# Linear attention feeding a gated FFN on one core: the order of every engine's instructions is chosen by the Tile scheduler instead of being the order of emission

## Chip, cores and metric

One NeuronCore of one Trainium2 chip runs the whole program. The metric is the device time of one execution in microseconds (us), lower is better. The profile is one execution taken by the hardware profiler.

## What is computed

Eight batches of eight heads, 576 tokens, head size 64, go through linear attention; the result, 4608 tokens of 512 features, goes through a feed-forward block whose two first products are multiplied element by element.

```
phi(x) = where(x > 0, x, exp(x) - 1) + 1
kv  = einsum('bhsd,bhse->bhde', phi(k), v);   z = sum over s of phi(k)
x   = einsum('bhsd,bhde->bhse', phi(q), kv) / (phi(q) . z + 1e-6)     # then (4608, 512)
out = (((x @ w1) * (x @ w2)) @ w3) @ w_out                            # 512 -> 1024 -> 1024 -> 512
```

Inputs and output are float32.

## The kernel before, in words

The matmuls run in bfloat16. Since nothing stands between `w3` and `w_out`, the kernel first forms their product `wf` (1024 x 512) on the chip: eight times `wf_unit` (eight transposes into the PSUM tile w3p, a copy to `w3t` on ScalarE, eight matmuls into `wf_ps`, a copy out on ScalarE).

Attention goes batch by batch. `load_qkv` brings k, v and q of a batch (1 MB each plus two small pieces for the last 64 tokens) through SyncE's queue (SP) into a pool `ld` of six buffers, which the float32 weights use too. `phi_steps` computes phi: two Exp instructions on ScalarE (line 127), two minima on VectorE (line 128), then four and one scalar_tensor_tensor on VectorE (lines 133 and 138) that write kj and kr, or qj and qr; the pool of these has one buffer each. `v_steps` casts v into `vt` on VectorE. `kv_unit` multiplies phi(k) with v (20 matmuls into `kvp`) and VectorE writes `kvz`; `tr_unit` (three parts) transposes phi(q) into `tp`, and VectorE copies it to `qt`; `nd_unit` (four) and `ndr_unit` (one, for the last 64 tokens) form numerator and denominator in `nd`; `nd_finish` computes exp(-ln(d)) in two ScalarE instructions (lines 230 and 231) and multiplies on VectorE (line 232) into `xt`, the transposed input of the FFN. kvp, tp, nd and w3p share a PSUM pool of two buffers (`at`).

The FFN goes in nine chunks of 512 tokens. `f_unit(c, f)`, written F(c,f) below, with f from 0 to 7, makes four matmuls into `a_ps` and four into `b_ps` (line 265), a copy of a_ps on ScalarE (line 268) and a product on VectorE into `ab` (line 269). `o_unit(c, m)`, written O(c,m), with m from 0 to 3, makes eight matmuls of ab with wf into `o_ps` (line 275), a copy on ScalarE (line 278) and a store from SP's queue (lines 282 and 285). a_ps, b_ps, o_ps and wf_ps share a PSUM pool of four buffers (`mm`).

Chunk c can start when all the columns of xt that it reads are written; the attention of batch c+1 is emitted among the units of chunk c, and the phi steps of batch c+2 between the later units. Up to chunk 5 this is the pattern. Chunk 6 still holds the attention of the last batch, but no phi steps; chunks 7 and 8 hold F and O units alone. The order written by hand for a chunk is:

```
units = [F(0), KV, F(1), O(0), T(0), T(1), F(2), T(2), O(1), F(3), N(0), F(4), N(1),
         O(2), F(5), N(2), F(6), N(3), NR, O(3), F(7)]      # O(m) is of chunk c-1
```

The beginning is written out too: weights of the product wf, then batch 0, then F(0,0) to F(0,7) with the phi steps of batch 1's k and its v cast between the last four, then the q steps of batch 1, its kv and tr units, O(0,m) and nd units in turn, and then the loads of batch 2 followed by all its phi steps, before F(1,0).

Line 75 sets `tc.manual_schedule()`: the instructions of each engine, and the DMAs on SP's queue, stand in the order in which this Python code emits them. Each engine takes its own list in order and waits at an instruction until that one's inputs and buffers are there. Semaphores between engines are generated from the data dependencies.

Of the kernel before, what the change touches and what calls it, by code (L numbers as in the profile page):

```python
# [18 lines left out]
def kernel(  # L19
# [52 lines left out]
    mm_ps = ctx.enter_context(tc.tile_pool(name="mm_ps", bufs=4, space=bass.MemoryType.PSUM))  # L72
    at_ps = ctx.enter_context(tc.tile_pool(name="at_ps", bufs=2, space=bass.MemoryType.PSUM))

    ctx.enter_context(tc.manual_schedule())
    nc.scalar.preload_act_table_set("natural_log_exp_and_others")

    ident = consts.tile([P, P], BF16)
# [377 lines left out]
```

## Time and profile before

| | |
|---|---|
| median of 3 runs | 342.56 us (342.13 to 477.45) |
| profiled execution, its own time | 344.31 us |
| its span, first to last instruction | 342.5 us |
| TensorE busy with matmuls (PE) | 278.5 us, 81% |
| VectorE (DVE) | 172.8 us, 50% |
| ScalarE (ACT) | 155.2 us, 45% |
| GpSimd (POOL) | 12.5 us, 4% |
| mean granted TensorE clock | 0.893 of full speed |
| read from HBM, written to it | 38.80 MB, 9.44 MB |

The span is 1.8 us shorter than the profiled execution's own time, since the time has work around the first and last instruction in it. Matmuls are pipelined, so a busy PE may still run at half its clock; the granted clock has to be read beside it. One execution of the three was far slower than the other two.

### The profile page before, as it was taken

Reading aid. Unit: us, or ns where it says so; the run is one execution under the profiler, and the core shown is the slowest. Engines: PE = TensorE matmul, PEld = TensorE weight load, DVE = VectorE, ACT = ScalarE, POOL = GpSimd, SP = SyncE. Lnnn points to the kernel's source line nnn. Section 1 sums busy time; section 2 is a strip of 40 time slices with the busy share of each in tenths; the row PEclk is TensorE's granted clock in tenths of the full one; section 3 lists DMA queues with packets and bytes.
Section 4 is the critical chain, followed back from the end, with each engine's and each line's share of the span. In section 5 each row is a group of like instructions: output and inputs, shape, how many; then the busy total and the mean of one; then the engine's idle time right before and its main releaser. Section 6 shows DMA issues by size and latency. Waiting matters only on the chain.

```text
span 342.5 us, 3960 instructions
## 1 busy us (share of the span) xinstructions
PE 278.5 (81%) x1440; PEld 128.6 (38%) x1440; DVE 172.8 (50%) x306; ACT 155.2 (45%) x237; POOL 12.5 (4%) x26
## 2 busy tenths in 40 slices
PE   1747484986962894998899699969988999999995
PEld 0223241434421441443354245424433544444442
DVE  1235264389226888349356935873494444232220
ACT  2153506270533395169228633942692256333332
POOL 2400430000000000000000000000000000000000
PEclk9989865795886797899699989989998999999999
DMA  7999953000179992020194049108700002010123
GB/s 267 398 356 380 373 154 124 2 2 0 61 225 363 325 298 94 3 61 31 41 324 142 33 146 330 34 30 265 243 31 31 33 31 61 33 62 32 63 61 122
DMA packets 47539, 48.49 MB, mean 142 GB/s; under 512 B 14240, under 2 KB 38816, under 8 KB 47520
## 3 DMA queue, kind: packets, MB, share of 16 engines
q1 hardware_dynamic: 47520, 48.24, 42.6%
q8 instruction: 11, 0.18, 0.2%
q14 instruction: 8, 0.07, 0.1%
HBM read 38.80 MB, written 9.44 MB: 141 GB/s over the span
## 4 chain that ended last, share of the span: by engine, by line
PE 74%; DVE 11%; ACT 6%; DMA 5%; issue 3%; SPq 0%; DVEq 0%; ACTq 0%
PE o_ps L275 20%; PE a_ps L265 19%; PE b_ps L265 18%; PE wf_ps L298 5%; PE nd L238 3%; PE kvp L182 3%; DVE qj L133 3%; DMA w<-in_moe_w_out_dram 3%; PE tp L211 2%; ACT w3t L295 2%; DMA k<-in_k_dram 2%; ACT e L127 2%; DVE xt L232 2%; PE kvp L188 1%; DVE ab L269 1%
## 5 line engine op out<-in xcount | busy, mean ns | idle before, releaser
L265 PEld LDWEIGHTS <-w_sb 128*128 128x128 bf16 x576 | 58.1, 103 | 77.9 <-issue 17.0
L269 DVE TENSOR_TENSOR ab<-a_sb,b_ps 128x512 bf16<-128x512 f32 x72 | 49.2, 684 | 75.4 <-PE b_ps L265 75.4
L265 PE MATMUL a_ps<-xt,w_sb 128*128 128x512 bf16 x288 | 81.2, 408 | 4.1 <-DVE xt L232 2.3
L265 PE MATMUL b_ps<-xt,w_sb 128*128 128x512 bf16 x288 | 77.5, 393 | 0.1
L275 PE MATMUL o_ps<-wf_sb,ab 128*128 128x512 bf16 x288 | 74.5, 408 | 0.0
L268 ACT COPY a_sb<-a_ps 128x512 f32<-128x512 f32 x72 | 41.9, 582 | 61.2 <-PE a_ps L265 55.4
L278 ACT COPY o_sb<-o_ps 128x512 f32<-128x512 f32 x36 | 21.0, 584 | 59.4 <-PE o_ps L275 59.4
L275 PEld LDWEIGHTS <-ab 128*128 128x128 bf16 x288 | 28.7, 103 | 35.4 <-issue 6.5
L230 ACT ACTIVATE r<-nd,eps 128x512 f32<-128x512 f32 (+1 forms) x40 | 25.7, 644 | 23.5 <-PE nd L248 13.0
L232 DVE TENSOR_TENSOR xt<-nd,r 128x512 bf16<-128x512 f32 (+1 forms) x40 | 25.3, 633 | 19.7 <-ACT r L231 19.5
L128 DVE TENSOR_SCALAR e<-e 128x1152 bf16<-128x1152 bf16 x32 | 14.4, 454 | 36.9 <-ACT e L127 36.8
L298 PE MATMUL wf_ps<-wo_sb,w3t 128*128 128x512 bf16 x64 | 20.3, 460 | 14.4 <-ACT w3t L295 12.3
L231 ACT ACTIVATE r<-r 128x512 f32<-128x512 f32 (+1 forms) x40 | 23.5, 587 | 1.3
L182 PE MATMUL kvp<-vt,kj 128*128 128x130 bf16 x128 | 15.5, 251 | 10.4 <-DVE vt L163 10.4
L238 PE MATMUL nd<-qt,kvz 128*128 128x512 bf16 x64 | 20.5, 409 | 2.9 <-DVE xt L232 2.3
L133 DVE SCALAR_TENSOR_TENSOR qj<-q,e 128x512 bf16<-128x512 f32 x32 | 21.6, 724 | 0.3
L133 DVE SCALAR_TENSOR_TENSOR kj<-k,e 128x512 bf16<-128x512 f32 x32 | 20.9, 685 | 0.2
L127 ACT ACTIVATE e<-q 128x1152 bf16<-128x1152 f32 x16 | 18.2, 1157 | 5.2 <-DMA q<-in_q_dram 5.2
L127 ACT ACTIVATE e<-k 128x1152 bf16<-128x1152 f32 x16 | 18.2, 1163 | 5.1 <-DMA k<-in_k_dram 5.1
L248 PE MATMUL nd<-qt,kvz 128*128 128x64 bf16 x64 | 3.7, 209 | 18.2 <-DVE xt L232 18.1
L298 PEld LDWEIGHTS <-w3t 128*128 128x128 bf16 x64 | 6.4, 110 | 25.1 <-ACT w3t L295 14.9
L182 PEld LDWEIGHTS <-kj 128*128 128x128 bf16 x128 | 9.2, 109 | 15.9 <-DVE vt L163 8.4
(39 smaller groups left out, 131.8 us busy)
## 6 DMA issues: line engine op xcount, KB each, us to landing
w<-in_moe_w_dram SPq DMA_DIRECT2D x8, 1024.0 KB, 9.3
k<-in_k_dram SPq DMA_DIRECT2D x8, 1024.0 KB, 7.1
v<-in_v_dram SPq DMA_DIRECT2D x8, 1024.0 KB, 7.9
q<-in_q_dram SPq DMA_DIRECT2D x8, 1024.0 KB, 7.0
out_dram<-o_sb SPq DMA_DIRECT2D x32, 256.0 KB, 2.3
w<-in_moe_w_out_dram SPq DMA_DIRECT2D x2, 1024.0 KB, 8.5
k<-in_k_dram SPq DMA_DIRECT2D x16, 64.0 KB, 6.4
v<-in_v_dram SPq DMA_DIRECT2D x16, 64.0 KB, 6.4
```

The source lines that it names most:

```text
L127: nc.scalar.activation(out=e[:, s], in_=x[:, s], func=AF.Exp)
L133: nc.vector.scalar_tensor_tensor(out=dst_j[:, j, :].rearrange("p (h d) -> p h d", h=H), in0=xj, scalar=1.0, in1=ej, op0=ALU.add, op1=ALU.max)
L182: nc.tensor.matmul(o, kj[:, j, hp * P:(hp + 1) * P], vt[:, j, 2 * hp:2 * hp + 2, :].rearrange("p h e -> p (h e)"), start=(j == 0), stop=False)
L230: nc.scalar.activation(out=r, in_=d_ap, func=AF.Ln, bias=eps[:, 0:1])
L231: nc.scalar.activation(out=r, in_=r, func=AF.Exp, scale=-1.0)
L232: nc.vector.tensor_tensor(out=dst, in0=n_ap, in1=r, op=ALU.mult)
L238: nc.tensor.matmul(nd[:, i, :], t[:, hp, i, :], qt[:, hp, 0:NJ * P], start=True, stop=True)
L265: nc.tensor.matmul(ps, w[:, kc, f * P:(f + 1) * P], xt[:, kc, cs], start=(kc == 0), stop=(kc == KC - 1))
L268: nc.scalar.copy(out=a_sb, in_=a_ps)
L269: nc.vector.tensor_mul(out=abs_[c][:, f, :], in0=a_sb, in1=b_ps)
L275: nc.tensor.matmul(o_ps, ab[:, f, m * P:(m + 1) * P], wf_sb[:, f, :], start=(f == 0), stop=(f == FC - 1))
L298: nc.tensor.matmul(ps, w3t[:, kc, :], wo_sb[:, kc, :], start=(kc == 0), stop=(kc == FC - 1))
```

## The change

The line that fixes the order is taken out. The Tile scheduler then chooses the order at build time: engine by engine, it takes among the instructions whose inputs it reckons to be ready, and for whose tile a buffer is free, the one that was emitted earliest, with the start times that its own model of durations gives. The lists that come out are fixed in the program: at run time each engine still takes its list in order. Tiles, pools, buffer numbers, instructions and their shapes are the same.

```
@@ -72,7 +72,7 @@
     mm_ps = ctx.enter_context(tc.tile_pool(name="mm_ps", bufs=4, space=bass.MemoryType.PSUM))
     at_ps = ctx.enter_context(tc.tile_pool(name="at_ps", bufs=2, space=bass.MemoryType.PSUM))
 
-    ctx.enter_context(tc.manual_schedule())
+    pass
     nc.scalar.preload_act_table_set("natural_log_exp_and_others")
```

## Rows read from the trace of the kernel before

**Rows 1.** The page, parts 1 and 2: busy time, and two lines in 40 slices.

```profile
PE 278.5 (81%) x1440; PEld 128.6 (38%) x1440; DVE 172.8 (50%) x306; ACT 155.2 (45%) x237; POOL 12.5 (4%) x26
...
PEclk9989865795886797899699989989998999999999
DMA  7999953000179992020194049108700002010123
```

**Rows 2.** The chain that ended last, in order of time: start, duration, what.

```profile
59.66 1.89 PE a_ps L265 x4
...
134.70 1.71 PE a_ps L265 x4
...
168.38 1.71 PE a_ps L265 x4
...
262.22 1.06 PE a_ps L265 x4
...
288.39 0.86 PE a_ps L265 x4
...
331.56 6.92 PE o_ps L275 x32
```

**Rows 3.** Windows by stage: stretch, its length, busy by engine, then clock, DMA share, GB/s.

```profile
59.66:98.38 38.72, 32.50 (x152) 14.83 (x153) 22.03 (x42) 16.81 (x26) 0.00 (x0) 0.81 0.09 31
98.38:134.70 36.32, 22.56 (x113) 10.04 (x113) 26.26 (x50) 17.27 (x23) 0.00 (x0) 0.79 0.93 290
134.70:168.38 33.68, 30.34 (x154) 13.82 (x152) 20.36 (x37) 16.99 (x27) 0.00 (x0) 0.85 0.08 25
168.38:199.66 31.28, 27.94 (x154) 13.12 (x152) 19.38 (x35) 16.69 (x26) 0.00 (x0) 0.94 0.47 147
...
230.94:262.22 31.28, 27.94 (x153) 13.12 (x152) 19.38 (x35) 16.69 (x26) 0.00 (x0) 0.94 0.45 147
262.22:288.39 26.17, 26.16 (x153) 12.65 (x152) 10.86 (x17) 12.78 (x22) 0.00 (x0) 1.00 0.12 41
```

**Rows 4.** Timeline of the beginning: start, duration, engine, instruction, idle before and its releaser.

```profile
18.84 4.30 SPq L107 DMA_DIRECT2D q<-in_q_dram  x2
...
36.22 2.29 POOL L361 CAST w_sb<-w 128x512 bf16<-128x512 f32 x4 [23.22 <-DMA w<-in_moe_w_dram]
...
38.56 2.22 ACT L127 ACTIVATE e<-q 128x1152 bf16<-128x1152 f32 x2
...
41.74 3.59 PE L298 MATMUL wf_ps<-wo_sb,w3t 128*128 128x512 bf16 x8 [3.25 <-ACT w3t L295]
```

**Rows 5.** DMA issues by line: size of one, median us from issue to landing.

```profile
q<-in_q_dram SPq DMA_DIRECT2D x8, 1024.0 KB, 7.0
```

**Rows 6.** Waits of SP's queue: us in total, times, longest.

```profile
SPq L102 <- DVE qr L138: 7.1, 1, 7.1
```

**Rows 7.** Timeline from the end of chunk 0 to the start of chunk 1.

```profile
78.51 0.37 PE L182 MATMUL kvp<-vt,kj 128*128 128x130 bf16 x2 [2.49 <-DVE vt L163]
...
96.26 0.39 SPq L102 DMA_DIRECT2D k<-in_k_dram  x1
...
98.38 1.65 PE L265 MATMUL a_ps<-xt,w_sb 128*128 128x512 bf16 x4 [2.31 <-DVE xt L232]
...
103.02 2.22 ACT L127 ACTIVATE e<-k 128x1152 bf16<-128x1152 f32 x2 [5.14 <-DMA k<-in_k_dram]
...
109.26 0.40 PE L182 MATMUL kvp<-vt,kj 128*128 128x130 bf16 x2 [7.52 <-DVE vt L163]
...
110.45 2.22 ACT L127 ACTIVATE e<-q 128x1152 bf16<-128x1152 f32 x2 [5.22 <-DMA q<-in_q_dram]
```

**Rows 8.** Timeline of the end of chunk 3.

```profile
192.51 1.90 DVE L133 SCALAR_TENSOR_TENSOR qj<-q,e 128x512 bf16<-128x512 f32 x3
...
195.86 0.68 DVE L232 TENSOR_TENSOR xt<-nd,r 128x512 bf16<-128x512 f32 x1
...
196.60 0.39 PE L248 MATMUL nd<-qt,kvz 128*128 128x64 bf16 x8 [3.34 <-DVE xt L232]
```

More of the change, by code (lines that the diff above doesn't have):

```diff
@@ L73 @@
     at_ps = ctx.enter_context(tc.tile_pool(name="at_ps", bufs=2, space=bass.MemoryType.PSUM))
-    ctx.enter_context(tc.manual_schedule())
+    pass
     nc.scalar.preload_act_table_set("natural_log_exp_and_others")
```

## Prediction

> **What bounds the kernel now.** I read the page first. PE is busy for 81% of the span, VectorE for 50%, ScalarE for 45% [rows 1]: TensorE sets the pace, and no other engine is near full. But the busy share is not evenly spread, and neither is the granted clock: the PEclk line falls to 5 in the seventh slice (51 to 60 us) and to 5 and 6 near 94 and 103 us, and has 9s at the end [rows 1]. The DMA line is full up to about 43 us, empty from about 60 to 86, and full again from 94 to 128 [rows 1]: loads stop in the middle of the ramp and then come in a burst.
>
> Next the chain that ended last, which is PE nearly throughout. I use it as a ruler. F(c,7) closes each written-out chunk, and its a_ps starts at 134.70 (c = 1), 168.38 (2), then at 262.22 (5) and 288.39 (6) [rows 2]; 199.66 and 230.94 lie between. Windows cut at these points show what a chunk costs [rows 3]. From 262.22 to 288.39 the work is eight F, four O and one batch's attention, and PE is busy for 26.16 of 26.17 us at clock 1.00. The chunks before it (168.38 to 199.66, 230.94 to 262.22) hold the same PE work, 152 weight loads in each, and take 31.28 us at 0.94. What differs is the phi steps: VectorE is busy 19.38 us in the one kind and 10.86 in the other. So 26.17 us is what a chunk costs PE when nobody keeps it waiting, at full clock: the a_ps group of four starts there takes 0.86 us, against 1.71 at 134.70 and 168.38 [rows 2], which are the 2.4 and 1.2 GHz levels.
>
> Then the ends of the waits. At the end of chunk 3, VectorE runs qj steps from 192.51 and the xt product that nd waits for only at 195.86; PE waits 3.34 us for it with ndr_unit [rows 8], O(2,3) and F(3,7) standing behind it. The 5.11 us lost per chunk (31.28 less 26.17) are this wait and some 1.8 us of low clock behind it, so a waited microsecond costs 5.11/3.34 = 1.53. In the ramp the same happens in a larger way: kv_unit(1) waits 2.49 us, F(1,0) 2.31, and kv_unit(2), which stands right behind F(1,0), 7.52 us for batch 2's v cast, while F(1,1) could have run [rows 7]. The k load of batch 2 is issued at 96.26 and its Exp begins at 103.02, after ScalarE waited 5.14 us [rows 7]; the load stood in SP's list behind chunk 0's stores, while DMA had been idle for over 20 us [rows 1].
>
> **The change, part by part.** It removes no instruction and adds none; the cost lies in positions alone. I sum on the profiled execution's span, 342.5, in which its own time is 344.3.
>
> *(a) Start, to F(0,0) at 59.66 [rows 2].* Batch 0's q is issued from 18.84 to 23.14 [rows 4]; with the median landing of 7.0 us [rows 5] it is there by about 30. Its Exp runs at 38.56, behind the copies of the wf units in ScalarE's list [rows 4]; and the last wf unit waits 3.25 us because that Exp stands ahead of its copy [rows 4]. Taken when it is ready, the Exp starts 8.5 us earlier. Batch 0's kv matmuls, whose k and v are there by then, need not stand between the wf units and the transposes; I count 2 us for that. Together -10.5, so F(0,0) at about 49. Bounds: 0, if the load order holds it; and -21, since the first half of w2 is cast from 36.22 to 38.5 [rows 4] and no F can end before.
>
> *(b) 59.66 to 98.38, F(0,0) to F(1,0).* Eight F, four O, one attention: the content of the 26.17 us chunk, in 38.72 us [rows 3]. The loads of batch 1 move with (a): q or v waits 7.1 us in SP's list for a buffer that batch 0's qr step frees [rows 6]. I take 31.5, nearer to the undisturbed row than the middle (32.4), because PE's waits are for order alone, and not at it because F(0,0) starts from a cold clock: -7.2. Bounds -12.5 and 0.
>
> *(c) 98.38 to 134.70.* Seven F and an attention, no O: 26.17 less one F (1.73, twice 0.86) and four O (6.92, the last row of the chain [rows 2]) makes 17.5 us, in 36.32 [rows 3]. Batch 2's k needs a buffer that a cast of w2 frees before 39 us [rows 4]; without its place behind the stores it can be issued as soon as batch 1's loads are, tens of microseconds before 96.26. Then neither the 5.14 nor the 7.52 us remain [rows 7]. I take 19.5: -16.8. Bounds -18.8 and -5.
>
> *(d) 134.70 to 262.22, four chunks of 33.68 and three times 31.28 [rows 3].* In the scheduler's order an xt product, emitted earlier than the phi steps, goes ahead of them as soon as it is ready, and a PE that waits for one unit takes the next. I take 28 for each, between 26.17 and 31.28 and nearer to the former, since VectorE's 19.4 and ScalarE's 16.7 us fit into 28 with room: -5.7 and three times -3.3, in sum -15.5. Bounds -22.8 and 0.
>
> A rule of the Trainium skill speaks against (d). The page Perfetto Trace Analysis, section Optimization Strategy, says that consistent bubbles, the same gap repeating on the engine that should be saturated, can mean too little SBUF or PSUM for the next tile. The 3.34 us gap [rows 8] does repeat, and the nd tile has two buffers; by that rule no order removes it, and (d) would give 2.4 us in place of 15.5. The forecast sides with the row, in which VectorE holds the buffer that long only because qj steps go first.
>
> *(e) 262.22 to the end.* PE is undisturbed (26.16 of 26.17), then F and O until 331.56 plus 6.92, a copy and a store: 0. If the scheduler mixes units, matmuls of one group may stand apart and wait for signals one by one; no row shows that. Bounds 0 and +3, the latter a tenth of the 31 us chunk of today; I take 0.
>
> *Sum:* -10.5 - 7.2 - 16.8 - 15.5 = -50.0, so 344.3 becomes 294.3. The median before lies 1.75 below the profiled time, and I expect the same after: 292.6, rounded up to 294 for small waits that I can't see.
>
> **The rivals.**
> *Gaps of the steady chunks stay* (buffers, not order, or bursts of phi on VectorE as before): (a) and (b) as above, (c) 17.5 + 5.1 = 22.6, -13.7, (d) only 33.68 to 31.28, -2.4. Sum -33.8: 310 against 344.3, 309 as a median. For it: nd's chain from ScalarE to VectorE is long and has two buffers. Against it: VectorE is 62% busy in these chunks.
>
> *The order comes out nearly as it was.* Earliest-emitted-first is the written order wherever all is ready; then 342. Against it: the waits of rows 7 are exactly where something else was ready.
>
> *Slower: lists built on loads that land later than reckoned.* The order is fixed before the run. If an Exp of phi is placed soon after its load is issued, ScalarE stands at it until the data lands, and the copies of a_ps behind it wait; four mm buffers hold two F units, 3.46 us, then PE stops. In the ramp this costs 5.14 and 5.22 us for one batch's k and q already today [rows 7]. If it met each of batches 1 to 6 or 2 to 7 in full, 10.4 us per batch, and (a) gained nothing: 26.17 + 10.4 in (b), 17.5 + 10.4 in (c), 36.6 in each chunk of (d): -2.2, -8.4, +2.9, +15.9, together +8, or 350; with 1.53 for the low clock, 15.9 per batch, +41, or 383. I put it at 358. It decides from 9.0 us lost per batch (54.2 us lost today between 59.66 and 262.22, over six batches), that is from 5.9 us waited. For it: an eager order asks for phi as soon as it can. Against it: six load buffers are two batches, and a batch is needed only once in 26 us, so in steady chunks a load has over three times its 7 us.
>
> **How the numbers follow.** The forecast, 294, has a chance of 0.56 with its own range from 278 to 306 (278 is (b) to (d) at their lower bounds with (a) as taken: 344.3 - 10.5 - 12.5 - 18.8 - 22.8 - 1.75; 306 is three quarters of the sum). Gaps stay, 306 to 335: 0.14. No change: 0.09. Slower: 0.21. The range runs from 278 to 350: 0.04 lies below, some 0.15 above. Two per cent, about what a measurement of this kernel can tell from no change, are 335.7 and 349.4: faster 0.70, within 0.09, slower 0.21.
>
> **What would show it.** (a): F(0,0) near 49, q's Exp near 30. (b), (c): batch 2's loads before 65 us, DMA no longer empty from 60 to 86, F(1,0) near 80, no wait of PE near 7 us there. (d): windows of some 28 us per chunk with 152 weight loads, clock near 1.0, xt products ahead of phi steps, phi steps spread over the chunk. The slower rival would show as ScalarE waiting for k and q loads over 5 us per batch, and copies of a_ps late behind them. The prediction is wrong if PE's idle time moves to other waits of the same length: partly filled a_ps groups that hold all four mm buffers while xt is unfinished, or transposes that hold the two at buffers before nd gets one.

## The result, and the profile after

The changed kernel takes 288.46 us (median of four executions, 287.31 to 290.66) against 343.09 for the kernel before: a ratio of 0.842, with a 95% interval from 0.836 to 0.849. That median takes in one execution at 477.45 us, which the ratio leaves out. The profiled execution took 288.92 us; its span is 287.1.

The page of the changed kernel, parts 1 and 2:

```profile
PE 259.0 (90%) x1440; PEld 123.4 (43%) x1440; DVE 170.3 (59%) x306; ACT 153.1 (53%) x237; POOL 11.0 (4%) x26
...
PEclk9996885999979999999999999999999999999999
DMA  7999999900699922889679521010011101100222
```

The counts on every engine are those of [rows 1]. Of the 55.4 us that are gone from the span, PE's busy time fell by 19.5 only (278.5 to 259.0, the same matmuls at a higher clock); 36 us were idle time. From the thirteenth slice on the clock line holds nothing but 9s.

The waits of PE, first in the kernel before (engine, line, what it waited for; us in total, times, longest):

```profile
PE nd L248 <- DVE xt L232: 18.1, 6, 3.8
PE wf_ps L298 <- ACT w3t L295: 12.3, 7, 3.2
PE kvp L182 <- DVE vt L163: 10.4, 4, 7.5
```

and in the changed kernel:

```profile
PE w3p L293 <- DVE w3b L318: 10.5, 2, 6.6
PE nd L248 <- DVE xt L232: 2.9, 3, 2.1
...
PE wf_ps L298 <- ACT w3t L295: 1.7, 3, 0.7
```

Three waits that held 40.8 us are down to 4.6; the third of them is not in the second list at all. One grew: the transposes of w3 now wait 10.5 us for a cast behind a weight load, where they waited 6.4.

Windows of the changed kernel by the same cuts as [rows 3], from F(1,0) to F(1,7) and then from each F(c,7) to the next:

```profile
82.50:98.88 16.38, 16.37 (x83) 7.19 (x82) 13.95 (x26) 10.64 (x15) 0.00 (x0) 0.90 1.09 348
...
98.88:128.69 29.81, 27.12 (x164) 13.03 (x162) 26.64 (x51) 21.95 (x35) 0.00 (x0) 1.00 0.57 167
128.69:155.05 26.36, 26.14 (x154) 12.71 (x153) 20.19 (x39) 18.27 (x28) 0.00 (x0) 1.00 0.87 265
155.05:181.03 25.98, 25.97 (x153) 12.61 (x152) 19.18 (x36) 16.43 (x26) 0.00 (x0) 1.00 0.36 108
...
207.01:233.00 25.99, 25.98 (x154) 12.63 (x152) 11.20 (x19) 12.64 (x22) 0.00 (x0) 1.00 0.12 41
```

The fourth row is the one to look at beside the fifth. A chunk with phi steps (VectorE 19.18 us) now takes 25.98 us, as long as one without them (25.99), and PE is busy for all but 0.01 of it. In [rows 3] the two kinds stood 5.11 us apart.

How that looks at one place, the end of chunk 3, in the timeline of the changed kernel (start, duration, engine, instruction; in brackets the idle time before it and its releaser). It answers to [rows 8]:

```profile
143.16 2.49 DVE L133 SCALAR_TENSOR_TENSOR qj<-q,e 128x512 bf16<-128x512 f32 x4
...
147.24 0.69 DVE L232 TENSOR_TENSOR xt<-nd,r 128x512 bf16<-128x512 f32 x1
...
152.18 0.69 DVE L232 TENSOR_TENSOR xt<-nd,r 128x512 bf16<-128x512 f32 x1 [0.57 <-ACT r L231]
...
152.93 0.39 PE L248 MATMUL nd<-qt,kvz 128*128 128x64 bf16 x8 [0.22 <-DVE xt L232]
```

The four qj steps of one batch are done 7 us ahead of `ndr_unit`'s matmul at 152.93, which waits 0.22 us in place of 3.34. In these chunks PE's units stand in the same order as the written one; it is VectorE's list that differs around them.

The beginning, in the timeline (it answers to [rows 4] and [rows 7]):

```profile
33.14 1.93 ACT L295 COPY w3t<-w3p 128x1024 bf16<-128x1024 bf16 x2
34.21 3.63 PE L298 MATMUL wf_ps<-wo_sb,w3t 128*128 128x512 bf16 x16 [0.71 <-ACT w3t L295]
34.95 1.18 ACT L127 ACTIVATE e<-q 128x1152 bf16<-128x1152 f32 x1
...
37.67 0.39 PE L182 MATMUL kvp<-vt,kj 128*128 128x130 bf16 x4
...
46.84 0.55 SPq L102 DMA_DIRECT2D k<-in_k_dram  x1
...
49.45 0.63 PE L265 MATMUL a_ps<-xt,w_sb 128*128 128x512 bf16 x1
...
80.27 0.39 PE L182 MATMUL kvp<-vt,kj 128*128 128x130 bf16 x4 [0.20 <-DVE xt L232]
...
82.50 1.87 PE L265 MATMUL a_ps<-xt,w_sb 128*128 128x512 bf16 x4 [0.21 <-DVE xt L232]
```

The wf units go in pairs: two copies to w3t back to back, then sixteen matmuls, and the Exp of q behind the copies. Batch 2's k is loaded at 46.84 instead of 96.26, and `kv_unit(2)`, which PE takes at 80.27 ahead of F(1,0), does not wait for data. Not all of batch 2 is early, though: the two small pieces of its v and its q still go out behind chunk 0's first stores, at 72.66 and 74.04.

### The profile page after: what moved, and what is told of

It is laid out like the page before. It is cut to its first block, busy times and chain, and to the rows that moved or that the text cites. A ratio compares the mean times of both kernels' runs of the same rounds, so it can differ in the third digit from the quotient of the medians.

```text
span 287.1 us, 3964 instructions
## 1 busy us (share of the span) xinstructions
PE 259.0 (90%) x1440; PEld 123.4 (43%) x1440; DVE 170.3 (59%) x306; ACT 153.1 (53%) x237; POOL 11.0 (4%) x26
## 4 chain that ended last, share of the span: by engine, by line
PE 67%; DVE 13%; DMA 7%; ACT 6%; issue 4%; SPq 1%; POOL 0%; DVEq 0%; ACTq 0%
PE a_ps L265 18%; PE b_ps L265 17%; PE o_ps L275 16%; PE wf_ps L298 5%; PE nd L238 3%; DMA w<-in_moe_w_out_dram 3%; PE kvp L182 3%; DVE qj L133 2%; DMA q<-in_q_dram 2%; PE tp L211 2%; DVE kj L133 2%; ACT e L127 2%; DVE xt L232 2%; DMA k<-in_k_dram 2%; PE kvp L188 1%
## 5 line engine op out<-in xcount | busy, mean ns | idle before, releaser
L265 PEld LDWEIGHTS <-w_sb 128*128 128x128 bf16 x576 | 56.0, 99 | 68.7 <-issue 6.3
L265 PE MATMUL a_ps<-xt,w_sb 128*128 128x512 bf16 x288 | 76.8, 384 | 1.7 <-DVE ab L269 1.4
L265 PE MATMUL b_ps<-xt,w_sb 128*128 128x512 bf16 x288 | 75.8, 383 | 0.3 <-ACT a_sb L268 0.3
L275 PE MATMUL o_ps<-wf_sb,ab 128*128 128x512 bf16 x288 | 68.1, 379 | 0.0
L275 PEld LDWEIGHTS <-ab 128*128 128x128 bf16 x288 | 27.1, 98 | 30.7
L298 PE MATMUL wf_ps<-wo_sb,w3t 128*128 128x512 bf16 x64 | 18.9, 449 | 2.7 <-ACT w3t L295 1.7
L133 DVE SCALAR_TENSOR_TENSOR kj<-k,e 128x512 bf16<-128x512 f32 x32 | 20.9, 685 | 0.1
L133 DVE SCALAR_TENSOR_TENSOR qj<-q,e 128x512 bf16<-128x512 f32 x32 | 19.9, 686 | 0.1
L293 PE MATMUL w3p<-ident,w3b 128*128 128x128 bf16 x64 | 6.0, 266 | 10.5 <-DVE w3b L318 10.5
L295 ACT COPY w3t<-w3p 128x1024 bf16<-128x1024 bf16 x8 | 7.7, 1015 | 10.1 <-PE w3p L293 10.1
L182 PE MATMUL kvp<-vt,kj 128*128 128x130 bf16 x128 | 12.7, 222 | 0.2 <-DVE xt L232 0.2
```

The source lines that it names most:

```text
L133: nc.vector.scalar_tensor_tensor(out=dst_j[:, j, :].rearrange("p (h d) -> p h d", h=H), in0=xj, scalar=1.0, in1=ej, op0=ALU.add, op1=ALU.max)
L182: nc.tensor.matmul(o, kj[:, j, hp * P:(hp + 1) * P], vt[:, j, 2 * hp:2 * hp + 2, :].rearrange("p h e -> p (h e)"), start=(j == 0), stop=False)
L265: nc.tensor.matmul(ps, w[:, kc, f * P:(f + 1) * P], xt[:, kc, cs], start=(kc == 0), stop=(kc == KC - 1))
L275: nc.tensor.matmul(o_ps, ab[:, f, m * P:(m + 1) * P], wf_sb[:, f, :], start=(f == 0), stop=(f == FC - 1))
L298: nc.tensor.matmul(ps, w3t[:, kc, :], wo_sb[:, kc, :], start=(kc == 0), stop=(kc == FC - 1))
```

## The experiments

The question behind the size of the gain is what an "order" is that costs 50 us: one engine's list, or how several lists stand to each other. Where an expectation names a theory by its letter, A is that the order on VectorE and ScalarE alone makes the gap of [rows 8] (qj steps ahead of the xt product); B is that PE's own order makes it (PE stands at a unit while the next one is ready); D is that no list is wrong by itself, and the gap is the mismatch of two fixed ones.

The first six runs fix the order of emission on some engines and leave the others to the scheduler. The edit is one line of the changed kernel, with the engines named in braces:

```diff
-    pass
+    ctx.enter_context(tc.manual_schedule(engines={mybir.EngineType.PE}))
```

**only_pe_fixed**, `{PE}`:

> TensorE keeps the written order; VectorE, ScalarE, GpSimd and SP's queue are the scheduler's. Theory A (PE waited because of what stood ahead of its inputs on VectorE, ScalarE and SP, not because of its own order): almost all of the gain stays, 290 to 300 us, chunk pace 26 to 27 us, and only the beginning gives some back. Theory B (PE's freedom to take another unit while one waits is the gain): 315 us or more, the chunk pace back near 31 us.

Measured: 305.03 us, 0.884 [0.879, 0.890] of the kernel before.

**dve_act_fixed**, `{DVE, Activation}`:

> VectorE and ScalarE keep the written order; TensorE, GpSimd and SP's queue are the scheduler's. Theory A: the chunk pace goes back to about 31 us (four chunks, some 17 to 20 us) and most of the gain in the beginning goes, 315 to 330 us. Theory B: 290 to 300 us, since PE can still take other units. Theory C (two buffers of the PSUM pool at set the gap of a chunk, whatever the order): pace as in the changed kernel.

Measured: 307.89 us, 0.893 [0.886, 0.899].

**only_sp_fixed**, `{SP}`:

> Only SP's queue keeps the written order, so batch 2's loads stand behind chunk 0's stores. Theory A: chunk pace 26 us, F(1,0) and chunk 1 later by 6 to 12 us, 295 to 302 us. If the place of the loads is worth nothing: 287 to 290 us.

Measured: 301.58 us, 0.874 [0.868, 0.880].

**only_sp_free**, `{PE, DVE, Activation, Pool}`:

> All engines keep the written order, only the DMAs of SP's queue are placed by the scheduler. Theory A: the 7.5 us wait of kv_unit(2) and the waits for batch 2's loads go, with little else, so 10 to 15 us are won of the kernel before: 328 to 334 us, chunk pace still 31 us. If the loads alone were the cause: under 310 us.

Measured: 335.78 us, 0.973 [0.966, 0.980].

**pe_dve_fixed**, `{PE, DVE}`:

> TensorE and VectorE keep the written order, ScalarE, GpSimd and SP's queue are the scheduler's. Theory D (the 5 us lost per chunk come from TensorE's and VectorE's written lists together: ndr_unit stands before O(c-1,3) and F(c,7) on one, its buffer's xt product behind qj steps on the other): pace back at 31 us, four chunks cost some 20 us again, 322 to 332 us. If either list or ScalarE's could make the gap: pace as with one group fixed, 26 to 27 us, 305 to 312 us.

Measured: 324.28 us, 0.938 [0.932, 0.944].

**pe_act_fixed**, `{PE, Activation}`:

> TensorE and ScalarE keep the written order, VectorE, GpSimd and SP's queue are the scheduler's. Theory D: VectorE can still put xt products ahead of phi steps, so the pace stays 26 to 27 us and the time near that of TensorE alone fixed, 303 to 312 us. If ScalarE's list is as much a part of the gap as VectorE's: pace 29 to 31 us, 318 us or more.

Measured: 317.35 us, 0.916 [0.910, 0.921], between the two ranges that were expected. Its stages below are those of an execution of 320.3 us, 3 us above the median.

To see where each of them wins, I cut every trace at two points, the first kv matmul of batch 2 and that of batch 7. The first part is the beginning, the second holds five chunks, and what follows batch 7's is PE-bound and the same everywhere (76.6 to 77 us, in dve_act_fixed 78.0). Windows between the two points (in only_sp_free 0.15 us behind the first and 0.1 behind the second), one row from each kernel; columns as in [rows 3]. The kernel before:

```profile
109.26:265.70 156.44, 136.85 (x728) 63.77 (x729) 101.01 (x184) 83.88 (x129) 0.00 (x0) 0.90 0.44 140
```

The changed kernel:

```profile
80.27:210.30 130.03, 126.89 (x736) 60.99 (x736) 99.96 (x184) 83.35 (x131) 0.00 (x0) 0.99 0.56 171
```

only_pe_fixed:

```profile
94.69:226.25 131.56, 126.95 (x729) 61.20 (x728) 96.11 (x174) 78.25 (x125) 0.00 (x0) 0.97 0.49 152
```

dve_act_fixed:

```profile
97.53:226.64 129.11, 121.92 (x712) 58.52 (x711) 99.04 (x182) 78.06 (x123) 0.00 (x0) 0.99 0.46 142
```

pe_dve_fixed:

```profile
99.91:246.01 146.10, 131.11 (x715) 62.58 (x730) 100.69 (x184) 81.28 (x126) 0.00 (x0) 0.93 0.41 129
```

only_sp_free:

```profile
106.77:258.29 151.52, 133.18 (x730) 62.60 (x729) 100.69 (x184) 81.18 (x126) 0.00 (x0) 0.93 0.39 122
```

Divided by five, a chunk costs 31.3 us before, 26.0 after, 26.3 with PE alone fixed, 25.8 with VectorE and ScalarE fixed, 29.2 with PE and VectorE fixed, and 30.3 with only SP free. The counts of weight loads differ by up to 25 of 736, since in some orders the first F units stand before the cut, and the first chunks still feel the beginning. From one F(c,7) to the next, in the steady chunks alone, a chunk costs 31.28 us before, 25.98 after and with PE alone fixed, 26.5 to 26.8 with VectorE and ScalarE fixed, 30.02 with PE and VectorE fixed, 27.9 with PE and ScalarE fixed, and 31.28 with only SP free. So theory A falls: with VectorE's and ScalarE's lists exactly as before, the steady chunks are within 0.9 us of the changed kernel's. Theory B falls by the same reading of only_pe_fixed, in which PE's list is exactly as before. Most of the gap is there only when PE's list and VectorE's both stay fixed. The totals of only_pe_fixed and dve_act_fixed were missed for the same reason: I had looked for the loss in the chunks, and it is in the beginning, where batch 2's kv begins at 94.69 and 97.53 instead of 80.27.

What each free side does is seen at the end of a chunk. In dve_act_fixed VectorE still runs its qj steps ahead of the xt product, but PE has other work in between:

```profile
167.66 1.90 DVE L133 SCALAR_TENSOR_TENSOR qj<-q,e 128x512 bf16<-128x512 f32 x3
...
168.24 1.89 PE L275 MATMUL o_ps<-wf_sb,ab 128*128 128x512 bf16 x8
...
169.96 1.03 PE L265 MATMUL a_ps<-xt,w_sb 128*128 128x512 bf16 x4
...
171.00 0.69 DVE L232 TENSOR_TENSOR xt<-nd,r 128x512 bf16<-128x512 f32 x1
...
171.75 0.39 PE L248 MATMUL nd<-qt,kvz 128*128 128x64 bf16 x8 [0.33 <-DVE xt L232]
```

The O unit and all but two matmuls of the F unit that used to stand behind `ndr_unit` have moved ahead of it and fill the 3.34 us. In pe_dve_fixed, with both lists frozen, the wait is back:

```profile
176.47 1.90 DVE L133 SCALAR_TENSOR_TENSOR qj<-q,e 128x512 bf16<-128x512 f32 x3
...
179.82 0.68 DVE L232 TENSOR_TENSOR xt<-nd,r 128x512 bf16<-128x512 f32 x1
...
180.56 0.39 PE L248 MATMUL nd<-qt,kvz 128*128 128x64 bf16 x8 [2.36 <-DVE xt L232]
...
181.00 3.04 PE L275 MATMUL o_ps<-wf_sb,ab 128*128 128x512 bf16 x7
```

With PE and VectorE fixed, the free ScalarE, GpSimd and SP help little (29.2 us a chunk against 31.3). In pe_act_fixed a chunk costs some 28 us, and `ndr_unit` still waits 12.5 us for xt there, in six times, against 15.5 in pe_dve_fixed and 18.1 before:

```profile
176.39 1.90 DVE L133 SCALAR_TENSOR_TENSOR qj<-q,e 128x512 bf16<-128x512 f32 x3
...
179.74 0.68 DVE L232 TENSOR_TENSOR xt<-nd,r 128x512 bf16<-128x512 f32 x1
...
180.47 0.39 PE L248 MATMUL nd<-qt,kvz 128*128 128x64 bf16 x8 [1.93 <-DVE xt L232]
```

So a free VectorE is not enough by itself: its list, chosen by the scheduler, has qj steps ahead of the xt product once more, though ScalarE has finished that product's input at 177.77. ScalarE's list is the third one in the chain from nd to xt, so I read this as a VectorE that can't place its steps freely while ScalarE's Exps stay where they are; no run tests that by itself.

The two runs on SP: with SP alone fixed, the load of batch 2's k goes out at 77.72, behind stores again, and ScalarE waits for k 5.9 us in four times; kv of batch 2 begins at 91.23, 11 us later than in the changed kernel, and the median is 13 us longer. With SP alone free, that load goes out at 51.78 and yet F(1,0) starts at 101.00, behind 98.38 before: early data is worth little while the lists that use it stay put. Of the 7.5 us that its span is shorter, 2.6 lie ahead of batch 2's kv and 4.9 in the first two chunks behind it; the steady ones are as they were.

**spread_by_hand.** If D is right, the gap goes with a hand-written order too, with every list fixed, the same buffers, and no scheduler. This is the kernel before, with the phi steps handed out one at a time instead of two in the late places:

```diff
-                    run(pq[:2] if i > 7 else pq[:1])
-                    del pq[:2 if i > 7 else 1]
+                    run(pq[:1])
+                    del pq[:1]
```

> The kernel before, all orders still written by hand, but one phi step behind each later unit of a chunk instead of two, so that VectorE's list has no run of qj steps ahead of an xt product. Theory D: the pace falls from 31 to 27 us or less though nothing is left to the scheduler and the buffers are the same, 342 - 4 x 4.5 = 322 to 328 us. If the two buffers of the pool at make the gap: 338 to 345 us.

Measured: 321.42 us, 0.928 [0.923, 0.934]. The window between nearly the same two points (the first kv matmuls stand at 110.25 and 243.62), and PE's waits:

```profile
110.85:243.81 132.96, 126.44 (x716) 61.00 (x729) 98.92 (x180) 83.58 (x129) 0.00 (x0) 0.97 0.51 163
```

```profile
PE kvp L182 <- DVE vt L163: 10.9, 4, 8.0
...
PE nd L248 <- DVE xt L232: 2.8, 2, 1.8
```

Two lines of Python take the 18.1 us of waits for the nd tile to 2.8, and a chunk to 26.7 us. The beginning is as before, with its 8.0 us wait for batch 2's v cast. That is 24 of some 55 us; the rest lies ahead of batch 2.

**spread_and_early_loads.** The same, with batch 2's loads issued right behind batch 1's q instead of behind chunk 0's stores, and its k and v phi steps between the O and nd units:

```diff
+    for n, s in (("k", k), ("v", v), ("q", q)):
+        load_qkv(n, s, 2)
...
+            prep2 = k_steps(2) + v_steps(2) + q_steps(2)
...
+                run(prep2[2 * m:2 * m + 2])
...
-            for n, s in (("k", k), ("v", v), ("q", q)):
-                load_qkv(n, s, 2)
-            run(k_steps(2) + v_steps(2) + q_steps(2))
+            run(prep2[8:])
...
```

> All orders written by hand: the phi steps spread as in spread_by_hand, batch 2's loads emitted behind batch 1's instead of behind chunk 0's stores, and the phi steps of batch 2's k and v between the O(0,m) and nd units instead of behind them. Theory D says that the rest of the loss is the same kind of thing in the ramp: the wait of kv_unit(2) (8.0 us in spread_by_hand) goes and kv_unit(2) runs near 98 us instead of 110.85, 306 to 312 us. If only a list made with foresight of durations can do it: 317 us or more.

Measured: 310.99 us, 0.904 [0.897, 0.910]. The load goes out at 50.50, and kv of batch 2 begins at 105.34 instead of 110.25, later than hoped: F(1,0) now waits 3.48 us for the last xt product, which stands on VectorE (101.50) behind the kj steps and v casts that I put ahead of it. With 127.29 us between the two points the chunks are at the undisturbed pace. What is left to the changed kernel, 22 us, is the beginning alone.

**attention_first.** The rest of the runs ask whether the beginning can be shorter still. Here the scheduler is free, but the order of emission is another one: batch 0's attention and the weights of F first, the product wf behind F(0,3):

```diff
...
-    w3r[0] = load_w(moe_w3, 0, 2, 0, DFF)
...
+    load_qkv("k", k, 0)
...
+    for f in range(4):
+        f_unit(0, f)
...
+    for i2 in range(4):
+        t = cast_w3(i2)
+        wf_unit(2 * i2, t[:, 0, :])
+        wf_unit(2 * i2 + 1, t[:, 1, :])
...
```

> The changed kernel with another order of emission in the beginning: batch 0's k, q and v and w1 and w2 are loaded first, then w3 and w_out, and the product wf is emitted behind F(0,3). In the changed kernel TensorE is half idle until F(0,0) at 49 us and has F(1,0) at 82; the work ahead of F(1,0) is some 50 us at full clock. If the order of the loads bounds the beginning: F(0,0) near 27 us, F(1,0) near 62 to 68, 268 to 275 us. If the latency of the chains bounds it: 283 to 290 us.

Measured: 289.14 us, 0.836 [0.833, 0.840] of the kernel before; the changed kernel has 0.842 [0.836, 0.849], so no difference is shown. F(0,0) starts at 28.64 instead of 49.45, and kv of batch 2 at 82.58 instead of 80.27.

**attention_first_f0**, the same with all eight F(0,f) ahead of wf:

```diff
-    for f in range(4):
+    for f in range(FC):
         f_unit(0, f)
...
```

> attention_first with all eight F(0,f) emitted ahead of the wf units instead of four, so that no F unit of chunk 0 is held back for the wf chain and batch 1's attention can stand between the wf units. If work at hand still bounds the beginning: kv_unit(2) near 75 to 78 us instead of 82.6, 281 to 285 us, faster than the changed kernel. If the sum of work and chains ahead of O(0,0) bounds it: 287 to 291 us, no better than the changed kernel (288).

Measured: 289.10 us, 0.843 [0.840, 0.846]. Windows of its beginning, cut at F(0,0), at the end of the F units, at the end of wf and at kv of batch 2:

```profile
0.00:28.46 28.46, 8.54 (x47) 4.25 (x48) 14.49 (x30) 8.13 (x9) 6.83 (x20) 1.00 0.97 352
28.46:44.50 16.04, 15.77 (x73) 7.09 (x74) 9.49 (x18) 7.98 (x14) 3.65 (x6) 1.00 0.95 352
44.50:66.40 21.90, 17.79 (x127) 9.84 (x128) 9.92 (x18) 15.62 (x19) 0.00 (x0) 1.00 0.58 190
66.40:81.29 14.89, 12.45 (x87) 6.48 (x88) 13.35 (x25) 10.14 (x17) 0.00 (x0) 1.00 0.46 151
```

and the beginning of the changed kernel in two windows, cut at F(0,0) and at kv of batch 2:

```profile
0.00:49.45 49.45, 30.91 (x174) 15.58 (x175) 21.98 (x41) 20.18 (x25) 11.01 (x26) 0.85 0.98 350
49.45:80.27 30.82, 28.44 (x164) 13.19 (x163) 26.16 (x50) 21.08 (x33) 0.00 (x0) 0.97 0.46 154
```

F(0,0) is 21 us earlier, the granted clock reads 1.00 from the start, and yet nothing is won. PE needs 54.5 us of busy time up to batch 2's kv instead of 59.3, and idles 26.7 us instead of 20.9. The idle time ahead of F(0,0) is as long as before, 19.9 us in 28.46 against 18.5 in 49.45, because the wf units no longer fill the time of the first loads (PE's first matmul, at 14.41, waits for batch 0's qj); another 4.1 us are lost among these units when they come later, between 44.50 and 66.40.

**mixed_start** and **mixed_start_late_wf** put one pair of wf units first and the others among the F units, or behind them:

```diff
...
+    wf_pair(0)
+    run(k_steps(0))
+    run(q_steps(0))
...
+    wf_pair(1)
+    for i in range(4):
+        cast_w(i)
+    for f in range(4):
+        f_unit(0, f)
+    wf_pair(2)
...
```

> The changed kernel with another order of emission in the beginning: loads w3 (first quarter), w_out, batch 0's k, q, v, then w1, w2 with the rest of w3 behind them; two wf units first, batch 0's attention next, the last four wf units among F(0,f). TensorE then has wf work while batch 0's attention waits for its chain, and F work while wf waits for ScalarE's copies. If the beginning is bound by which work is at hand: kv_unit(2) near 68 to 74 us instead of 80.3, 274 to 282 us. If the chains of copies and casts bound it whatever the order: 285 to 291 us.

Measured: 294.25 us, 0.855 [0.848, 0.862], above both ranges that were expected. F(0,0) starts at 47.3, and kv of batch 2 at 87.32.

For mixed_start_late_wf all eight F units go ahead of `wf_pair(2)` and `wf_pair(3)`, and the loads of the last two pairs of w3 go behind batch 1's k, v and q (the edit against mixed_start):

```diff
...
-    for f in range(4):
+    for f in range(FC):
         f_unit(0, f)
-    wf_pair(2)
...
+    wf_pair(2)
+    wf_pair(3)
```

> As mixed_start, but batch 1's k, v and q are loaded ahead of the second half of w3, and the last four wf units are emitted behind F(0,7) and the phi steps of batch 1's k. If the order of the loads still counts behind F(0,0): 3 to 6 us off mixed_start, since batch 1's attention no longer waits for its data behind w3; else the same as mixed_start within 2 us.

Measured: 296.27 us, 0.861 [0.854, 0.869]; the 3 to 6 us that it was to win over mixed_start did not come. Four orders of emission for the beginning, and none beats the one that was there. The last two read 2 and 2.7% longer than the changed kernel, the first of them with an interval that touches its own. What holds batch 2's kv at 80 us stays open. Up to F(0,0) the DMA engines are 98% busy in the changed kernel; from there on VectorE is busy for 26.16 of 30.82 us (85%). Either could set the end, and no run here took work from one of them. The late small pieces of batch 2's v are a third candidate: their cast ends at 80.42, and the first matmul that reads it starts at 80.58. By themselves they don't explain it, since in attention_first all of v has gone out by 54.3 and kv still begins at 82.58.

## Why the prediction was right, step by step

The forecast was 294 us and the measurement is 288.46. The sum of the terms was -50.0 on the profiled execution, and came out at -55.4 (344.31 to 288.92). Of the 5.4 us between the two, 3.9 are in (d). Two slips of the working do not enter the sum: the 5 of the PEclk line that I put near 94 us is the tenth slice, 77 to 86 us, and three quarters of the sum give 305 us, not 306.

*(a) Start, -10.5: measured -10.2*, F(0,0) at 49.45. The size was right and the working was not. I had q's Exp start 8.5 us earlier; it starts 3.6 earlier (34.95), and behind the copies of the wf units, not ahead of them. What pays is the opposite: the copies no longer stand behind each other's matmuls, since the wf units go in pairs. PE's wait for w3t falls from 12.3 us to 1.7, the one for w3b grows from 6.4 to 10.5, in sum 6.5 us less. Kv of batch 0 then begins at 37.67. I had read one wait of that kind, the last of 3.25 us [rows 4], and not that there were seven. So the agreement of (a) to 0.3 us is luck. Part of it is bookkeeping, too: ten attention matmuls that stood ahead of F(0,0) before, two of `nd_unit` and the eight of `ndr_unit`, now come behind its first one, and count in (b).

*(b) -7.2 and (c) -16.8: measured -5.7 and -19.9.* F(0,0) to F(1,0) takes 33.05 us, F(1,0) to F(1,7) 16.38. They are best taken together, because `kv_unit(2)` has moved from (c) into (b): -25.6 against -24.0. The mechanism is as predicted in the main: batch 2's k and most of its v are issued before 65 us (46.84 and 50.52), F(1,0) starts near 80 (82.50), and there is no wait of 7 us. The rest of v and q came later than I had it, behind chunk 0's first stores, and the DMA engines, which I expected no longer to be empty from 60 to 86, are 5% busy from 57.4 to 71.8. That (c) came out below the 17.5 us that I had worked out as its least is moved work, not faster work: it holds 83 matmuls against 113, since `kv_unit(2)` stands ahead of it and the last `nd_unit` and `ndr_unit` of batch 2 behind it. Both parts needed more than one free list: with SP's list fixed the loads are late again, with only SP's free they are early and not used.

*(d) -15.5: measured -19.4*, 98.88 to 207.01. The chunks take 29.81, 26.36, 25.98 and 25.98 us, where I had put 28 for each. This is the term that was mis-sized: I kept 1.8 us over the undisturbed row as a reserve for bursts of phi, and three of the four needed next to none. The first needed more. It has taken over the ten matmuls from (c), and in it the wait of [rows 8] comes back once, smaller: VectorE runs four qj steps ahead of an ab product that frees a mm buffer, and PE stands for 1.42 us.

```profile
101.69 2.49 DVE L133 SCALAR_TENSOR_TENSOR qj<-q,e 128x512 bf16<-128x512 f32 x4
...
104.42 0.69 DVE L269 TENSOR_TENSOR ab<-a_sb,b_ps 128x512 bf16<-128x512 f32 x1
...
105.16 1.02 PE L265 MATMUL a_ps<-xt,w_sb 128*128 128x512 bf16 x4 [1.42 <-DVE ab L269]
```

The price of a waited microsecond, 1.53, fits this gap: a 3.34 us wait less is 5.30 us less (31.28 to 25.98), or 1.59, with the clock at 1.00 in place of 0.94. It is no constant: in pe_act_fixed a 1.93 us wait costs 1.93 (27.91 against 25.98). The reason was half right. VectorE does run the xt product in time, but this isn't needed: it is enough that PE's list is free, or VectorE's and ScalarE's together, as dve_act_fixed and only_pe_fixed show, and so is another fixed order, as spread_by_hand shows.

*(e) 0: measured -0.2*, 207.01 to the end against 262.22 to the end.

The rivals. *Gaps stay* falls. The gap recurs once per chunk in the kernel before, and spread_by_hand removes 15.3 of its 18.1 us with the same two buffers, so order alone can close it. No run had a third buffer, so whether one would close it as well is not shown. The Trainium skill, page Perfetto Trace Analysis, section Optimization Strategy, reads consistent bubbles as a possible lack of SBUF or PSUM. Here the bubble is the late release of a buffer, queued behind other work in a list, and it went with the buffers unchanged. *Order as it was* falls by the chunks and by F(0,0). *Slower, by loads that land late*: in the changed kernel ScalarE waits for a q load 1.9 us and for a k load 0.7 us in all, once each, far from the 5.9 us per batch from which this was to decide. The partly filled a_ps groups that I had feared do occur: at 49.45 and 50.73 F(0,0) runs one matmul at a time between nd units. They cost nothing that the waits show there. In the wait at 105.16 they take part: F(2,0), begun at 102.05 and with six of its eight matmuls done, holds two of the four mm buffers while PE waits for one.

## What to carry to other kernels

When an engine waits at the same place in every round for an engine that is only 60% busy, look at what stands ahead of the releasing instruction in that engine's list and what stands behind the waiting one; moving either can remove the wait, so a small change to a hand-written order can be worth nearly as much in the steady part as a scheduler for all (26.7 against 26.0 us a chunk here). Look again afterwards: in pe_act_fixed the freed VectorE had the qj steps ahead of the xt product once more. Cut the trace at one and the same unit in a disturbed and an undisturbed round to see what the wait costs, clock included, before touching anything. The beginning is another matter: there the lists of loads, casts, copies and matmuls all have to move together, and leaving PE's, SP's or VectorE's and ScalarE's fixed delayed batch 2 by 11 to 17 us here.

## What the runs showed of the hardware

A low granted clock came with the longer of PE's waits. Chunks with the 3.34 us wait ran at 0.94 on average [rows 3] and the same chunks without it at 1.00; of the 5.30 us that such a chunk became shorter, 1.97 is PE's own busy time (27.94 to 25.97), which is the clock, and the rest the wait. In pe_dve_fixed a chunk with a 2.36 us wait also ran at 0.94 and took 30.02 us. In pe_act_fixed a chunk with a 1.93 us wait ran at 1.00 and took 27.91 us, 1.93 more than one without: there a wait cost its own length and no more.

```profile
185.93:215.95 30.02, 27.50 (x151) 13.03 (x152) 19.37 (x35) 16.76 (x26) 0.00 (x0) 0.94 0.17 56
184.15:212.06 27.91, 25.82 (x150) 12.60 (x152) 19.28 (x35) 16.68 (x26) 0.00 (x0) 1.00 0.15 47
```

(The first line is of pe_dve_fixed, the second of pe_act_fixed.) And a granted clock of 1.00 does not say that the matmuls run at full speed. attention_first_f0 has 1.00 through its first 81.29 us, where the changed kernel has 0.85 up to F(0,0), and yet four `nd_unit` matmuls take 1.89 us at the beginning, as long as the slow group at 59.66 in [rows 2], and 1.03 us later:

```profile
23.74 1.89 PE L238 MATMUL nd<-qt,kvz 128*128 128x512 bf16 x4 [1.45 <-DVE kvz L197]
...
74.11 1.03 PE L238 MATMUL nd<-qt,kvz 128*128 128x512 bf16 x4
```

So the length of a matmul has to be read beside the clock. Both kernels reach batch 2's kv within some 1 us of each other, because the busy time that attention_first_f0 saved turned into idle time.
